# Reordering the first transfers of a fused convolution and MLP kernel: softmax weights first on their own queue, x split on ScalarE's queue, the band read in 128 rows

## The chip, the cores and the metric

The kernel runs on one core of a Trainium2 chip. The metric is device time in microseconds: 745.34 us before, the median of three runs (745.31 to 746.46). A profiled execution of the same kernel took 745.89 us; its span from the first to the last instruction is 743.8 us, so 2.09 us lie around the span. TensorE's mean granted clock in it was 0.989. All times within the span below come from that execution.

## What is computed

A lightweight causal convolution along the sequence, whose seven taps per head are a softmax of a small weight table, followed by a two-layer MLP with an ELU between:

```python
# x: (8, 4096, 192) f32; weight: (8 heads, 7)
w = softmax(weight, axis=-1)
x_pad = concat([zeros(B, 6, D), x], axis=1)
attn[b, s, h, :] = sum_k w[h, k] * x_pad[b, s + k, h, :]      # 24 channels per head
h = attn.reshape(32768, 192) @ w_in                            # w_in (192, 2048)
g = where(h > 0, h, exp(min(h, 0)) - 1)
out = g @ w_out                                                # w_out (2048, 192), out f32
```

## The kernel before

The 32,768 tokens are cut into 32 super-tiles of 1,024 tokens, each of two groups of 512. A super-tile's d_ff is cut into 16 blocks q of 128; n counts blocks over all super-tiles, and each block has a unit for each group (r = 0, 1). For a unit, TensorE makes h in three matmuls of 64 rows (line 755), ACT takes the exponential (582), GpSimd clamps it (541), DVE combines it with h into gT (650), and TensorE multiplies by w_out (778) into an accumulator that ACT evacuates (586).

From super-tile 1 on, the convolution is a matmul of windows of x (xg, 118 rows for 112 outputs: 112 plus six of padding) with a banded matrix Tm (line 728). Its results csb are transposed by a DMA of SP into att. Tm is made once: the zeros zw go to a DRAM tensor `band` of 128 rows x 8 heads x 134 columns (line 812), the seven taps are written along its diagonals (822), and it is read back at an offset of six columns (827). The order on SP's queue is written out: zeros, diagonal, then the copy of w_in's second part from the upper 64 partitions to the lower 64 (825), then Tm. Waits stand between them: zeros after all of x for the first super-tile (`s_xs`), diagonal after the zeros and after DVE's wprb, copy after w_in's second part (`s_w[1]`), Tm after the diagonal.

Super-tile 0 is started differently, so as not to wait for Tm. Its x is loaded in float32 as windows of 112 rows (xs) by three DMAs in `first_window`: group 0's first window of 106 rows (the six of padding are zeroed by DVE) and its other four on SP, and group 1's five on ACT. ACT casts xs to xb in three steps (line 562); TensorE transposes xb (691), DVE and ACT evacuate to xT, and TensorE multiplies xT by seven diagonal matrices, taps (706), which DVE makes from the softmax (619). DVE and ACT evacuate to att.

The softmax weights wq arrive by three small DMAs on SP, behind its two loads of x: twice 64 rows by channel (lines 798), once a broadcast to all rows (806). DVE subtracts the maximum (596, 598), ACT takes the exponential wex (558), DVE normalises (605 to 609) and makes taps. On ACT, wex stands ahead of the casts xb. GpSimd issues all other loads: w_in's first part in six DMAs, its second part in three, w_out's first half, xg of super-tile 1, w_out's second half and xg of super-tile 2.

A planner in Python gives TensorE's order: each item has a planned time, from a clock per group that is held to at least 1,160 ns per block at the start (`PACE0`), and the items are sorted by it. `WARM = (15, 2)` are fillers, matmuls of 128 x 512 zeros without use: 15 stand before the transposes, and before each of n = 1, 2 and 3 stand two. Their count does not enter the planned times. The first convolution stands at n = 5 (`EARLY_CONV`), the first multiplication by w_out at n = 4 (`EARLY_O`). The second unit of a block from n = 4 on waits for the copy of w_in (`s_wd`).

Of the kernel before, what the change touches and what calls it, by code (L numbers as in the profile page):

```python
# [15 lines left out]
D = 192  # L16
# [3 lines left out]
CW = 112  # L20
GS = 512
SUP = 2 * GS
PAD = KSIZE - 1
KW = CW + PAD
TW = P + PAD
NWIN = 5
# [8 lines left out]
O_AT = (12, 16)  # L35
CONV_AT = (14, 18, 23, 25)
QB = 2
WARM = (15, 2)
WCOLS = ((0, 4 * FC), (4 * FC, 16 * FC))
XP = 128  # L40
MM_H, MM_O, MM_C = 216.0, 82.5, 102.5
# [12 lines left out]
def bass_lightweight_conv__then__act_elu_kernel(  # L54
# [80 lines left out]
    def emit(lists):  # L135
        at = [0, 0]
        while True:
            ready = [
                rt
                for rt in range(2)  # L140
                if at[rt] < len(lists[rt])
                and (lists[rt][at[rt]][2] is None or lists[rt][at[rt]][2]())
            ]
            if not ready:
                assert all(at[rt] == len(lists[rt]) for rt in range(2))
                return
            rt = min(ready, key=lambda rt: (clock[rt], 1 - rt))
            took, issue, _ = lists[rt][at[rt]]
            at[rt] += 1
            issue()  # L150
            clock[rt] += took
            if len(ready) == 1 and at[1 - rt] < len(lists[1 - rt]):
                clock[1 - rt] = max(clock)

    def warm(count):
        what = ("w", len(plan) + 1)
        take_bank(what)
        freed[bank_of[what]] = max(clock)
        plan.append((max(clock) - AHEAD, what + (count,)))
        clock[:] = [max(clock)] * 2  # L160
# [37 lines left out]
    for n in range(NP):  # L198
        if 0 < n < EARLY_O[0]:
            warm(WARM[1])  # L200
        if n < UNTIL:
# [32 lines left out]
    emit(tail)  # L234
    pe_order += [("w", 0, WARM[0])] + start_up
    pe_order += [item for _, item in sorted(plan, key=lambda p: p[0])]
# [38 lines left out]
    band = nc.dram_tensor("conv_band", (P, HEADS, TW), BF16).ap()  # L275

    with ExitStack() as stack:
        def sbuf(name, shape, dt):
            return stack.enter_context(nc.sbuf_tensor(name, shape, dt))
# [4 lines left out]
        def sema(name):  # L284
            return stack.enter_context(nc.semaphore(name))

        xg = sbuf("xg", [P, NXB, 2 * NWIN, D], BF16)
        Tm = sbuf("Tm", [P, HEADS, CW], BF16)
# [4 lines left out]
        xs = sbuf("xs", [P, 2 * NWIN, D], FP32)  # L293
# [28 lines left out]
        s_xs = sema("s_xs")  # L322
# [65 lines left out]
            W(s_fa, a)  # L388
            W(s_fd, d)

        def first_window(eng, gr, w0, w1):
            skip = PAD if gr + w0 == 0 else 0
            eng.dma_start(
                xs[skip:CW, 2 * w0 + gr : 2 * w1 : 2, :],
                bass.AP(
                    tensor=x_flat.tensor,
                    offset=(gr * GS + w0 * CW - PAD + skip) * D,
                    ap=[[D, CW - skip], [CW * D, w1 - w0], [1, D]],
                ),
            ).then_inc(s_xs, 16)  # L400

# [5 lines left out]
        def transposed(j):  # L407
            return xT[:, j, :].rearrange("p (w c) -> p w c", c=CW), windows_of(j)

        def first_att(j, c0, c1):  # L410
            b = bank_of["d", j] + (j == 2 and c0 > 0)
            return att[:, 0, j, c0:c1], H[:, b, c0:c1]
# [9 lines left out]
        def conv_evac(W, m):  # L422

            s, u = divmod(m, CU)
            if s > 2:
                W(s_att[s % 2], att_need(s - 2))
            return (
                csb[0:CW, s % 2, :].rearrange("p (r h i) -> p h r i", h=HEADS, i=8)[
                    :, HU * u : HU * (u + 1), :, :
                ],  # L430
                H[0:CW, bank_of["c", m], :]
                .rearrange("p (h c) -> p h c", h=HU)[:, :, 0:UC]
                .rearrange("p h (r i) -> p h r i", i=8),
            )
# [11 lines left out]
        def out_evac(W, k, g):  # L446
            W(s_out[k % 2], 32 * (k // 2))
            W(s_fin[g], k + 1)
            return (
                osb[:, k % 2, g, :, :].rearrange("p k d -> p (k d)"),  # L450
                acc_of(k, g)[:, 0 : 2 * D],
            )
# [97 lines left out]
        @block.scalar  # L550
        def _scalar(a):
            W = Waits(a)
            first_window(a, 1, 0, NWIN)
            a.memzero(scr[:, 0:1]).then_inc(s_scr)
            W(s_scr, 1)
            a.activation(scr[:, 1:2], scr[:, 0:1], ACT.Exp)
            W(s_set, 2)
            a.activation(wex[:], wq2[:], ACT.Exp).then_inc(s_wex)  # L558
            W(s_xz, 1)
            W(s_xs, 48)  # L560
            for j in range(3):
                a.activation(  # L562
                    xb[0:CW, j, :, :].rearrange("p w (h i) -> p w h i", i=8),
                    xs[0:CW, :, :].rearrange("p w (h j i) -> p j w h i", j=3, i=8)[:, j, :, :, :],
                    ACT.Copy,
                ).then_inc(s_cast)
            for sem, count, ins in (
                (s_xt, 3, transposed(2)),
                (s_first, 1, first_att(0, 0, GS)),
                (s_first, 3, first_att(2, 0, GS // 2)),  # L570
            ):
                W(sem, count)
                a.activation(*ins, ACT.Copy).then_inc(s_fa)  # L573
            for item in act_order:
                if item[0] == "c":
                    m = item[1]
                    W(s_cv, m + 1 - CU)
                    a.activation(*conv_evac(W, m), ACT.Copy).then_inc(s_ce)  # L578
                elif item[0] == "h":
                    i = unit_at[item[1:]]  # L580
                    W(s_h, i + 1)
                    a.activation(  # L582
                        E[:, i % NE, :], H[:, bank_of[item], :], ACT.Exp
                    ).then_inc(s_exp)
                else:
                    a.activation(*out_evac(W, *item[1:]), ACT.Copy).then_inc(s_oev[item[2]])  # L586
            evacuated_by(W, NK - 1, 1)
            out_group(a, NK - 1, 1)
# [203 lines left out]
        @block.sync  # L792
        def _sync(sy):
            W = Waits(sy)
            first_window(sy, 0, 0, 1)
            first_window(sy, 0, 1, NWIN)
            for g in range(2):
                sy.dma_start(  # L798
                    wq[HP * g : HP * (g + 1), HEADS, :],
                    bass.AP(  # L800
                        tensor=weight.tensor,
                        offset=0,
                        ap=[[KSIZE, HEADS], [0, HP // HEADS], [1, KSIZE]],
                    ),
                ).then_inc(s_wq, 16)
            sy.dma_start(
                wq[:, 0:HEADS, :].rearrange("p h k -> p (h k)"),
                bass.AP(tensor=weight.tensor, offset=0, ap=[[0, P], [1, HEADS * KSIZE]]),
            ).then_inc(s_wq, 16)
            W(s_zw, 1)  # L810
            W(s_xs, 48)
            sy.dma_start(
                band[:, :, :].rearrange("p h t -> p (h t)"), zw[:, :]
            ).then_inc(s_band, 16)
            W(s_band, 16)
            W(s_set, 6)
            diagonal = bass.AP(
                tensor=band.tensor,
                offset=0,
                ap=[[HEADS * TW + 1, P], [TW, HEADS], [1, KSIZE]],  # L820
            )
            sy.dma_start(diagonal, wprb[:, :, :]).then_inc(s_band, 16)
            W(s_w[1], 48)
            c0, c1 = WCOLS[1]
            sy.dma_start(w_in[HP:P, :, c0:c1], w_in[0:HP, :, c0:c1]).then_inc(s_wd, 16)
            W(s_band, 32)
            sy.dma_start(
                Tm[0:KW, :, :], band[0:KW, :, PAD : PAD + CW]
            ).then_inc(s_band, 16)

            sync_work = []
            for m in range(2 * CU - 1, CU * NS, CU):
                sync_work.append((unit_at_conv[m], ("c", m)))
            sync_work += [(at, item) for at, item in evacs]
            for _, item in sorted(sync_work):
                if item[0] == "c":
                    transpose(sy, W, item[1] // CU)
                elif item[1:] != (NK - 1, 1):
                    evacuated_by(W, *item[1:])
                    out_group(sy, *item[1:])  # L840
            for b in range(2):
                sy.wait_ge(s_out[b], 32 * NS)
# [28 lines left out]
```

## Time and profile before

| | us |
|---|---|
| Median of three runs | 745.34 |
| Profiled execution | 745.89 |
| Its span | 743.8 |
| TensorE's matmuls busy | 722.5 (97%) |
| ACT busy | 676.6 (91%) |
| GpSimd busy | 668.4 (90%) |
| DVE busy | 639.5 (86%) |
| First h product starts | 23.60 |
| First convolution starts | 36.94 |

Each busy time is that of one engine over the span; the engines work beside each other, so that the times are not to be added. The page also cuts the span into 40 slices of 18.6 us, and the digit is the busy share in tenths. The first two slices are where TensorE is not full:

```profile
PE   4599999999999999999999999999999999999998
PEclk7889999999999999999999999999999999999999
DMA  9616534445653644553354655344456435544212
```

The issues of the start, in time order, as the timeline has them (start, length of the issue on its engine): x on SP 0.80 (two, 0.78 together) and on ACT 0.80 (0.40), wq 1.62 (two, 1.43 together) and 3.08 (0.46), zeros 7.92, diagonal 18.16, copy of w_in 19.01, Tm 25.06. GpSimd issues its loads without a pause from 1.45 to 11.9.

### The profile page before, as it was taken

How to read it: one execution, taken by the hardware profiler on the slowest of the kernel's cores; microseconds unless marked ns; L12 is line 12 of the kernel's file. 1: busy time of each engine (PE TensorE's matmuls, PEld its weight loads, DVE VectorE, ACT ScalarE, POOL GpSimd, SP SyncE). 2: the span in 40 equal slices, each digit the busy share in tenths (PEclk: the TensorE clock that was granted, in tenths of full speed). 3: DMA queues.
4: the chain of work that ended last, by engine and by line, in shares of the span. 5: the costliest groups of instructions: out<-in, count | busy, mean ns of one | idle time of the engine just before them, and what ended most of it. 6: DMA issues, size and time to landing. Idle time of an engine off the chain costs nothing.

```text
span 743.8 us, 27548 instructions
## 1 busy us (share of the span) xinstructions
PE 722.5 (97%) x11823; PEld 681.0 (92%) x11824; DVE 639.5 (86%) x1044; ACT 676.6 (91%) x1285; POOL 668.4 (90%) x1111
## 2 busy tenths in 40 slices
PE   4599999999999999999999999999999999999998
PEld 1268999999999999999999999999999999999997
DVE  2479889899988989898998998898999889898993
ACT  2389999999999999999999999999999999999993
POOL 5379999999999999999999999999999999999893
PEclk7889999999999999999999999999999999999999
DMA  9616534445653644553354655344456435544212
GB/s 164 92 25 84 89 53 84 82 83 83 94 68 65 93 73 92 84 94 60 70 95 71 94 84 91 54 82 83 82 84 94 68 64 93 75 91 82 69 33 65
DMA packets 135800, 59.23 MB, mean 80 GB/s; under 512 B 100900, under 2 KB 135166, under 8 KB 135678
## 3 DMA queue, kind: packets, MB, share of 16 engines
q1 hardware_dynamic: 90814, 39.86, 23.5%
q0 software_dynamic: 44016, 16.99, 22.3%
q8 instruction: 92, 1.51, 0.8%
q10 hardware_dynamic: 848, 0.63, 0.3%
q14 instruction: 30, 0.25, 0.1%
HBM read 35.07 MB, written 25.45 MB: 81 GB/s over the span
## 4 chain that ended last, share of the span: by engine, by line
PE 91%; DMA 4%; POOL 2%; ACT 1%; DVE 1%; SPq 0%; issue 0%; DVEq 0%
PE H L778 51%; PE H L755 36%; PE H L728 3%; DMA Tm<-conv_band 2%; DMA wq<-in_weight_dram 1%; POOL E L541 1%; DMA conv_band<-wprb 1%; ACT E L582 1%; DVE gT L650 1%; POOL xg L481 0%; ACT csb L578 0%; SPq L798 0%; DVE xT L628 0%; DVE taps L619 0%; ACT osb L586 0%
## 5 line engine op out<-in xcount | busy, mean ns | idle before, releaser
L650 DVE SCALAR_TENSOR_TENSOR gT<-E,H 128x512 f16<-128x512 f32 x1024 | 633.4, 681 | 74.8 <-POOL E L541 73.1
L778 PE MATMUL H<-w_out,gT 64*128 64x192 f16 x8192 | 684.6, 243 | 0.1
L755 PE MATMUL H<-att,w_in 64*128 64x512 bf16 x3072 | 682.6, 377 | 0.4
L541 POOL TENSOR_SCALAR E<-E 128x512 f32<-128x512 f32 x1024 | 607.2, 612 | 62.1 <-ACT E L582 50.8
L778 PEld LDWEIGHTS H<-w_out,gT 64*128 64x128 f16 x8192 | 625.7, 94 | 22.3 <-PE H L778 2.2
L582 ACT ACTIVATE E<-H 128x512 f32<-128x512 f32 x1024 | 593.7, 601 | 37.3 <-PE H L755 11.5
L755 PEld LDWEIGHTS H<-att,w_in 64*128 64x128 bf16 x3072 | 275.8, 93 | 6.9 <-issue 1.5
L728 PE MATMUL H<-xg,Tm 64*112 64x240 bf16 x496 | 93.4, 268 | 8.0 <-DMA Tm<-conv_band 7.4
L578 ACT ACTIVATE csb<-H 112x480 bf16<-112x480 f32 x124 | 69.8, 563 | 0.0
L728 PEld LDWEIGHTS H<-xg,Tm 64*112 64x112 bf16 x496 | 58.5, 127 | 12.1 <-DMA Tm<-conv_band 7.7
L586 ACT ACTIVATE osb<-H 128x384 f32<-128x384 f32 x127 | 61.7, 486 | 7.5 <-PE H L778 7.4
L481 POOL DMA_DIRECT2D xg<-in_x_dram x63 | 56.1, 895 | 0.2 <-issue 0.2
L596 DVE TENSOR_REDUCE wmx<-wq 128x9 f32<-128x63 f32 x1 | 0.2, 220 | 12.2 <-DMA wq<-in_weight_dram 12.2
L558 ACT ACTIVATE wex<-wq 128x63 f32<-128x63 f32 x1 | 0.3, 256 | 11.4 <-DVE wq L598 11.4
L691 PE MATMUL H<-ident,xb 112*128 112x112 bf16 x15 | 1.8, 293 | 7.8 <-ACT xb L562 7.8
L685 PE MATMUL H<-zw 128*128 128x512 bf16 x20 | 7.6, 539 | 1.7 <-DVE zw L593 1.5
L691 PEld LDWEIGHTS H<-ident,xb 112*128 112x128 bf16 x15 | 1.2, 134 | 8.6 <-issue 8.3
L685 PEld LDWEIGHTS H<-zw 128*128 128x128 bf16 x21 | 2.4, 129 | 6.1 <-issue 4.6
L641 DVE COPY osb<-H 128x384 f32<-128x384 f32 x1 | 0.6, 559 | 8.5 <-PE H L778 8.5
L706 PE MATMUL H<-xT,taps 128*128 128x512 bf16 (+1 forms) x28 | 6.3, 393 | 0.2 <-DVE xT L628 0.2
L706 PEld LDWEIGHTS H<-xT,taps 128*128 128x128 bf16 x28 | 3.0, 111 | 3.4 <-issue 2.1
L573 ACT ACTIVATE att<-H 128x512 bf16<-128x512 f32 (+1 forms) x2 | 1.0, 490 | 5.2 <-PE H L706 5.2
(25 smaller groups left out, 19.8 us busy)
## 6 DMA issues: line engine op xcount, KB each, us to landing
out_dram<-osb SPq DMA_DIRECT2D x127, 192.0 KB, 3.3
xg<-in_x_dram POOLq DMA_DIRECT2D x61, 240.0 KB, 5.1
w_out<-in_moe_w_out_dram POOLq DMA_DIRECT2D x2, 384.0 KB, 16.7
w_in<-in_moe_w_in_dram POOLq DMA_DIRECT2D x3, 192.0 KB, 7.2
w_in<-w_in SPq DMA_DIRECT2D x1, 576.0 KB, 8.8
att<-csb SPq DMA_TRANSPOSE x31, 4.2
xs<-in_x_dram ACTq DMA_DIRECT2D x1, 420.0 KB
w_in<-in_moe_w_in_dram POOLq DMA_DIRECT2D x6, 64.0 KB, 5.5
```

What stands on the lines that cost most here:

```text
L481: g.dma_start(xg[0:rows, b, 2 * w0 + gr : 2 * w1 : 2, :], src).then_inc(s_x[b][gr], 16)
L541: g.tensor_scalar(out=E[:, i % NE, :], in0=E[:, i % NE, :], scalar1=1.0, scalar2=0.0, op0=ALU.min, op1=ALU.max,).then_inc(s_clp)
L578: a.activation(*conv_evac(W, m), ACT.Copy).then_inc(s_ce)
L582: a.activation(E[:, i % NE, :], H[:, bank_of[item], :], ACT.Exp).then_inc(s_exp)
L586: a.activation(*out_evac(W, *item[1:]), ACT.Copy).then_inc(s_oev[item[2]])
L650: v.scalar_tensor_tensor(out=gT[:, s % NG3, q, u, :], in0=E[:, i % NE, :], scalar=1.0, in1=H[:, bank_of[item], :], op0=ALU.subtract, op1=A ...
L685: pe.matmul(H[:, bank, :], zw[:, 0:P], zw[:, 0:GS], start=True, stop=True)
L691: ins = pe.matmul(windows_of(j)[:, w, :], xb[0:CW, j, 2 * w : 2 * w + 2, :].rearrange("p g c -> p (g c)"), ident[0:CW, 0:CW], start=w in ( ...
L706: ins = pe.matmul(H[:, bank_of[item] + part, c0:c1], taps[:, tap, :], xT[:, j, tap + c0 : tap + c1], start=(tap == 0), stop=(tap == KSIZE ...
L728: ins = pe.matmul(H[0:CW, bank_of["c", m], 256 * q : 256 * q + UC], Tm[rows, h, :], xg[rows, s % NXB, :, CPH * h : CPH * (h + 1)].rearrang ...
L755: ins = pe.matmul(H[:, bank_of[item[:3]], :], w_in[HP * r : HP * (r + 1), j, FC * q : FC * (q + 1)], att[HP * r : HP * (r + 1), s % 2, j, ...
L778: ins = pe.matmul(acc_of(k, g)[:, D * kb : D * (kb + 1)], gT[HP * rt : HP * (rt + 1), t % NG3, q, g, t0 : t0 + P], w_out[HP * rt : HP * (r ...
```

## The change

The transfers of x all go to ACT's queue, in four DMAs instead of three: group 0's first window is split into 96 rows and 10 rows, the other four windows and group 1's five stay whole. The three loads of the weights thereby are the first on SP's queue. The two waits for x count four DMAs instead of three. Tm is read in all its 128 rows instead of 118; the matmuls still use 118. The fillers before n = 1, 2 and 3 are one each instead of two.

```diff
-WARM = (15, 2)
+WARM = (15, 1)
...
-        def first_window(eng, gr, w0, w1):
-            skip = PAD if gr + w0 == 0 else 0
+        def first_window(eng, gr, w0, w1, r0, r1):
             eng.dma_start(
-                xs[skip:CW, 2 * w0 + gr : 2 * w1 : 2, :],
+                xs[r0:r1, 2 * w0 + gr : 2 * w1 : 2, :],
                 bass.AP(
                     tensor=x_flat.tensor,
-                    offset=(gr * GS + w0 * CW - PAD + skip) * D,
-                    ap=[[D, CW - skip], [CW * D, w1 - w0], [1, D]],
+                    offset=(gr * GS + w0 * CW - PAD + r0) * D,
+                    ap=[[D, r1 - r0], [CW * D, w1 - w0], [1, D]],
                 ),
             ).then_inc(s_xs, 16)
...
         def _scalar(a):
             W = Waits(a)
-            first_window(a, 1, 0, NWIN)
+            first_window(a, 0, 0, 1, PAD, PAD + 96)
+            first_window(a, 0, 0, 1, PAD + 96, CW)
+            first_window(a, 0, 1, NWIN, 0, CW)
+            first_window(a, 1, 0, NWIN, 0, CW)
...
-            W(s_xs, 48)
+            W(s_xs, 64)
             for j in range(3):
...
         def _sync(sy):
             W = Waits(sy)
-            first_window(sy, 0, 0, 1)
-            first_window(sy, 0, 1, NWIN)
             for g in range(2):
...
             W(s_zw, 1)
-            W(s_xs, 48)
+            W(s_xs, 64)
             sy.dma_start(
                 band[:, :, :].rearrange("p h t -> p (h t)"), zw[:, :]
             ).then_inc(s_band, 16)
...
             sy.dma_start(
-                Tm[0:KW, :, :], band[0:KW, :, PAD : PAD + CW]
+                Tm[:, :, :], band[:, :, PAD : PAD + CW]
             ).then_inc(s_band, 16)
```

## The prediction, made before the changed kernel was run

> **What bounds the kernel now.** I read the page first (engine shares and slices), then the chain that ended last in order of time, then the waits of the first 60 us, the busy time in stretches, and last the packets of each DMA queue in stretches of a microsecond. Bulk first: the row of busy time from 100 to 700 us (columns: length, busy time and instruction count of PE, PEld, DVE, ACT, POOL, then PEclk, DMA share, GB/s):
>
> ```profile
> 100.00:700.00 600.00, 599.91 (x10095) 581.42 (x10092) 541.92 (x879) 577.11 (x1099) 566.81 (x939) 1.00 0.48 80
> ```
>
> TensorE is busy for 599.91 of 600 us at full clock. The change edits nothing there, so what it is worth is by how much it moves the point at which this stretch begins. The chain shows what that point waits for (start, length):
>
> ```profile
> 3.08 10.75 DMA wq<-in_weight_dram
> 15.43 1.23 DVE taps L619 x7
> 16.66 1.29 DVE xT L628 x2
> 18.16 6.89 DMA conv_band<-wprb
> 25.06 11.84 DMA Tm<-conv_band
> 36.94 0.44 PE H L728
> ```
>
> Thirty of the first 37 us are three transfers: the softmax weights until 13.83, the taps written into the band in HBM, and the band read back as Tm. The waits say the same from the engines' side (total, times, longest):
>
> ```profile
> DVE wmx L596 <- DMA wq<-in_weight_dram: 12.2, 1, 12.2
> ACT wex L558 <- DVE wq L598: 11.4, 1, 11.4
> PE H L691 <- ACT xb L562: 7.8, 1, 7.8
> PE H L728 <- DMA Tm<-conv_band: 7.4, 1, 7.4
> SPq L358 <- DMA xs<-in_x_dram: 4.3, 1, 4.3
> SPq L358 <- DVE wprb L629: 9.8, 1, 9.8
> ```
>
> x has landed at 7.92 (SP goes on then, with the band's zeros), yet ACT starts its casts xb only at 14.53: they stand behind wex in its queue, and wex waits for the weights. TensorE loses 7.8 us there and 7.4 us before its first convolution. Why do 32 KB of weights take 10.75 us? The packets of SP's hardware queue in 8:9, 9:10 and 10:11 us, and then in 30:37 us, when Tm is read (packets, MB, share of 16 engines):
>
> ```profile
> q1 hardware_dynamic: 24, 0.00, 1.7%
> q1 hardware_dynamic: 7, 0.00, 0.4%
> q1 hardware_dynamic: 5, 0.00, 0.4%
> ...
> q1 hardware_dynamic: 929, 0.21, 13.5%
> ```
>
> A share of 13.5% of 16 engines is 2.2 engines: Tm's 118 rows x 8 heads = 944 pieces of 224 B run on two engines, 472 each, 25 ns apiece. And from 8 to 11 us only 36 small packets crawl, while the software queue holds the engines (92 to 108% in the same answers).
>
> [...]
>
> **The change part by part.**
>
> *Weights ahead.* SP loses two x issues (0.37 + 0.35) and starts wq at 0.80: issues of 0.79, 0.60 and 0.46 end near 2.7. x issued at 0.80 had its first packets just before 2.0, so the last wq transfer starts near 3.8 [...]. GpSimd's data begins between 4 and 5 (19 packets in that microsecond). I take 4.8; bounds 4.3 and 7. Then wmx and wq2 (0.25 each), wex (0.29), wsum, wrs, wch (0.77) end at 6.4, taps (1.23) at 7.6. Before, taps ended at 16.66.
>
> *x on ACT.* Four issues of 0.40 plus gaps run from 0.80 to 2.5; they delay the table load (1.28) and two tiny steps to 4.2, hidden as wex can't start before 5.3. The transfers are 96 + 10 + 448 + 560 = 1,114 pieces on one queue. ACT's queue moved 380 pieces in 3:4 us before, so 2.9 us from 2.0: read at 4.9, landed at 6.0 (bounds 5.3, and 9 if it meets the weights). The wait for 64 instead of 48 only counts the fourth transfer. Behind it on ACT are xb, xT and the first att; on SP the zeros, the diagonal, the w_in copy and Tm.
>
> *The start that follows.* xb runs 6.0 to 8.0 (1.97 before). TensorE's 15 fillers end at 7.6 as before, so the transposes run 7.6 to 8.5, xT on DVE and ACT to 9.4, the 21 full-size tap products from 8.7. Before they took 6.31 us, half of it at clock 0.50 after idling; now the fillers have just ended, so 21 x 0.216 = 4.5 us, to 13.3 (at the old speed 15.0). First h product: 13.6, against 23.6. w_in's first part must be there; GpSimd issues its last DMA at 4.38 and the trace has 10.3 us to landing, 14.7[...]. So 13.6 to 14.7.
>
> *WARM 2 to 1.* Three 512-column fillers of 0.216 go. One n took 1.29 and ACT's two exponentials 1.08, so n = 1 to 3 gain up to 0.6 us. I count it as nothing, since a wait follows directly (below); if none did, 0.6. The planner ignores the count, so the order stays.
>
> *Band and Tm.* Zeros issued at 6.3 instead of 7.92; landed near 9.7. wprb follows xT on DVE: 9.7. Diagonal issued near 10.2; its 1,024 pieces of 14 B took 6.89; against the larger w_in packets I say landed at 17.7 (bounds 16 and 20). In SP's order the copy of w_in to the lower half stands between, waiting for w_in's second part: 19.0 in the trace. The first two of its three loads were counted at 11.6 and 12.65 (issued 4.92 and 5.45, 6.7 and 7.2 to landing); [...] I take 15 (bounds 13.5 and 19). The copy (0.71 to issue) moves behind the diagonal [...]: landed 21.5 (23.8 by its old 8.8). Tm is issued at 17.7 to 18.4: [...]. **Tm lands at 24.5**; bounds 21.2 (issue + 3.5, nothing in its way) and 27. [...]
>
> *The sum.* TensorE needs the copy for the second h of n = 4, the first half of w_out before it (21.1 before, less now), and xg of super-tile 1 (22.3 and 23.9 before) plus Tm at the first convolution. By pace it arrives there at 13.6 + 5 x 1.1 = 19 to 20; so DMA still decides, at 24.5 against 36.94: **12.4 us gained**. The clock is down after the wait as before, so no gain from it. 743.8 - 12.4 = 731.4 us of span; with the 2.09 outside it 733.5; the profiled 745.89 is 0.55 above the median, so 733.0 for the median.
>
> **The rivals.**
> 1. *Likeliest: the SP chain w_in, copy, Tm decides*, 21.5 to 27 around 24.5: 733.0, own range 730.5 to 735.5. Chance 0.57.
> 2. *No long wait remains.* Everything lands with the pace, conv from about 21 and with a clock kept up (about half of the 4.4 us at 0.50 from 36.94 saved): 15.9 to 18 gained, 727.5 to 729.5. [...] 0.13.
> 3. *The start doesn't move much, only Tm gets short.* w_in and w_out bound the start, because GpSimd's queue is full until 24 us [...]. Tm issued at 25.06 would land at 28.6, before TensorE asks at 29.6: the 7.4 us go and about 2.2 of cold clock: 735.7 to 738. 0.22.
> 4. *Tm is not spread after all*: 18 + 11.84 = 30 or a little more: gain 6.5, 738.8. 0.02.
> 5. *Slower: x caught on its single queue.* [...] xb then starts when x lands; each microsecond beyond 14.53 costs one, but the 7.4 us of Tm's wait are returned, so it decides from x at about 22 us, and at 26 would give 749. Against: 1,022 of the same 1,114 pieces had moved by 5 us. 0.04.
> 6. *Nothing measurable*, gains and delays even out at 745: 0.02.
>
> **How the numbers follow.** 0.2% is 1.5 us, about what a measurement tells from no change. Faster is 0.57 + 0.13 + 0.22 + 0.02 = 0.94, the same 0.02, slower 0.04. From 729.5 to 737.5 takes in the first case with both bounds and most of the third; outside lie most of case 2, a part of 3, and 4 to 6, about two tenths.
>
> **What would show it.** Right: DVE's wmx before 7 us, xb near 6, first h product near 14, TensorE's first convolution between 21 and 27 with Tm or the w_in copy as releaser, Tm landing within 8 us of issue, SP's queue near 16 engines while it moves, 100 to 700 us unchanged. Wrong: wmx still after 10 us; w_in's second part still at 19 [...]; a new wait at xs; a second wait after the first convolution that gives the gain back.

## The result, and the profile after

The changed kernel takes 737.45 us (median of four runs, 737.37 to 737.84) against 745.33 us for the kernel before beside it: a ratio of 0.9892, 95% interval 0.9875 to 0.9909, or 7.9 us. Its profiled execution took 737.50 us with a span of 735.4 us, 8.4 less than before. A second set of runs on another chip gave 737.08 us and 0.9885 (0.9870 to 0.9899), that is 8.5 us.

The slices of the page, now 18.4 us each, that answer to those shown of before:

```profile
PE   5899999999999999999999999999999999999998
PEclk8899999999999999999999999999999999999999
DMA  9725545345566435345436464534445634544212
```

In the rows of TensorE and its clock only the first two slices differ. The long stretch is what it was, in the row of 100 to 700 us of the changed kernel (columns as before):

```profile
100.00:700.00 600.00, 599.92 (x10095) 580.99 (x10090) 542.11 (x878) 577.01 (x1098) 566.00 (x938) 1.00 0.48 80
```

So the whole gain is a shift of the start. The first convolution begins at 28.91 in place of 36.94 us, 8.0 earlier, and the span is 8.4 shorter. How the start gets there is told by the chain that ended last in the changed kernel (its main pieces; start, length):

```profile
2.48 9.38 DMA xs<-in_x_dram
11.95 5.83 DMA conv_band<-zw
17.80 7.01 DMA conv_band<-wprb
24.82 4.04 DMA Tm<-conv_band
28.91 0.31 PE H L730
```

Read it beside the chain of before. There the weights ended first (13.83), then the diagonal went out at 18.16 and Tm at 25.06. Now x heads the chain, and the diagonal goes out at 17.80 and Tm at 24.82: these two have hardly moved. What has changed is Tm's own time, 4.04 in place of 11.84 us. Some of the waits of the changed kernel up to 60 us, first the engines', then those of SP's queue (total, times, longest):

```profile
DVE wmx L598 <- DMA wq<-in_weight_dram: 6.5, 1, 6.5
PE H L693 <- ACT xb L564: 6.1, 1, 6.1
ACT wex L560 <- DVE wq L600: 3.8, 1, 3.8
ACT xb L564 <- DMA xs<-in_x_dram: 3.0, 1, 3.0
PE H L757 <- DMA w_in<-w_in: 1.8, 1, 1.8
```

```profile
SPq L358 <- DMA xs<-in_x_dram: 9.1, 1, 9.1
SPq L358 <- DVE wprb L631: 2.7, 1, 2.7
SPq L822 <- DMA conv_band<-zw: 2.7, 1, 2.7
```

The weights are there at 8.19 (wmx starts then; 13.86 before), but the casts xb now wait for x itself, which lands at 11.95 and not at 7.92 as before. On SP, the wait for x grew from 4.3 to 9.1 us, and after wprb was ready the diagonal still waited 2.7 us for the zeros. Last, TensorE waits 1.8 us for the copy of w_in at n = 4; Tm lands 1.3 us after that wait ends. In between TensorE has work, so that what it loses here it loses to the copy. In the profile of the second set, where the first convolution began at 27.84, the diagonal went out at 16.95, Tm at 23.72, and the chain itself goes through the copy instead of the diagonal and Tm:

```profile
17.39 9.29 DMA w_in<-w_in
```

Tm is indeed spread. The line below is SP's hardware queue in 26 to 28 us of the changed kernel (packets, MB, share of 16 engines); 0.26 MB in 981 packets means that nearly all of them are Tm's pieces of 224 B. The share of 69.8% is 11.2 of 16 engines; before, it was 13.5%, 2.2 engines, while Tm was read. How far the read in 128 rows would spread, no trace of before showed; it was the author's estimate, and the share is what was measured:

```profile
q1 hardware_dynamic: 981, 0.26, 69.8%
```

### The profile page after: what moved, and what is told of

Its sections match the earlier page's. It is cut to its first block, busy times and chain, and to the rows that moved or that the text cites. A ratio compares the mean times of both kernels' runs of the same rounds, so it can differ in the third digit from the quotient of the medians.

```text
span 735.4 us, 27543 instructions
## 1 busy us (share of the span) xinstructions
PE 721.5 (98%) x11820; PEld 680.7 (93%) x11821; DVE 640.4 (87%) x1044; ACT 676.9 (92%) x1285; POOL 668.3 (91%) x1111
## 3 DMA queue, kind: packets, MB, share of 16 engines
q10 hardware_dynamic: 1444, 1.05, 0.7%
## 4 chain that ended last, share of the span: by engine, by line
PE 92%; DMA 4%; POOL 2%; ACT 1%; DVE 1%; ACTq 0%; issue 0%; DVEq 0%; SPq 0%
PE H L780 52%; PE H L757 37%; PE H L730 4%; POOL E L540 1%; DMA xs<-in_x_dram 1%; DMA conv_band<-wprb 1%; ACT E L584 1%; DMA conv_band<-zw 1%; DMA Tm<-conv_band 1%; DVE gT L652 1%; POOL xg L480 0%; ACT csb L580 0%; ACTq L392 0%; ACT osb L588 0%; DVE osb L643 0%
## 5 line engine op out<-in xcount | busy, mean ns | idle before, releaser
L580 ACT ACTIVATE csb<-H 112x480 bf16<-112x480 f32 x124 | 69.8, 563 | 0.0
L687 PE MATMUL H<-zw 128*128 128x512 bf16 x17 | 6.0, 508 | 1.5 <-DVE zw L595 1.5
L498 POOL DMA_DIRECT2D w_in<-in_moe_w_in_dram x9 | 5.2, 652 | 0.1
```

The costliest lines, as they stand in the source:

```text
L498: g.dma_start(w_in[HP * half : HP * (half + 1), j, c0:c1], bass.AP(tensor=moe_w_in.tensor, offset=8 * j * FF + c0, ap=[[CPH * FF, HEADS], ...
L687: pe.matmul(H[:, bank, :], zw[:, 0:P], zw[:, 0:GS], start=True, stop=True)
```

## The experiments

Twelve runs in three sets of four; one of them is the changed kernel again. Each set ran on one chip, with the kernel before beside it: medians of 745.87, 746.35 and 745.61 us. Ratios are to that kernel.

### Each half alone

The kernel before, with one line changed:

```diff
-                Tm[0:KW, :, :], band[0:KW, :, PAD : PAD + CW]
+                Tm[:, :, :], band[:, :, PAD : PAD + CW]
```

> The kernel before, with Tm read in 128 rows as the only edit. Theory A (the short read of Tm is the whole gain, the reordering of the start nets nothing): Tm issued near 25.0, landed near 29, first convolution near 29.6, time 737.4 within 0.8 of the changed kernel. Theory B (the reordering gives a part of its own): 739 to 741, and the first convolution after 30.5.

Measured: 738.61 us, ratio 0.9903 (0.9886 to 0.9919).

The changed kernel with the same line put back:

> The changed kernel, with Tm read in 118 rows as before. Theory A: Tm issued near 24.8, some 11.8 us to landing, first convolution near 36.7, time 745 within 0.8 of the kernel before. Theory B: 742 to 744.

Measured: 742.24 us, 0.9950 (0.9936 to 0.9965), as theory B had it. The first of the two runs lies between the theories in time (738.61), and with B by its first convolution. The chain of the first of these two kernels:

```profile
18.13 7.08 DMA conv_band<-wprb
25.22 6.26 DMA Tm<-conv_band
31.52 0.31 PE H L728
```

and of the second:

```profile
17.16 6.60 DMA conv_band<-wprb
23.78 8.90 DMA Tm<-conv_band
32.73 0.45 PE H L730
```

The short read of Tm alone is worth 7.3 us, the reordering with its single filler alone 3.6, both together 7.9 to 8.5 (the two sets), not 10.9: the two shorten the same wait. With Tm short and the old order, Tm took 6.26 us from issue where the changed kernel has 4.04, and the copy of w_in ahead of it on SP landed at 28.4 (18.62 + 9.8).

That the reordering nets nothing is refuted for Tm in 118 rows (3.6 us). On top of the short Tm it is less sure: the first convolution comes 2.6 to 3.7 us earlier (31.52 against 28.91 and 27.84), but the time is only 1.2 to 1.5 us less, by comparing 738.61 with 737.45 and 737.08, and the intervals of the ratios overlap. The run with the short Tm alone has two fillers in each place, the changed kernel one; reordered with two (below) the medians are 736.81 and 736.34, 1.8 to 2.3 us less.

### Why x became late

Two suspects were tried: GpSimd's software queue, and the weights' small pieces ahead on SP. The first was taken away by holding GpSimd's loads until x is there:

```diff
+            W(s_xs, 64)
             load_w_in(0, 0)
```

> The changed kernel, with GpSimd's loads held until x has landed. If the software queue's early packets are what makes x land at 11.95 in place of 7.92, x lands by 7 us here; if it is the weights' tiny pieces in SP's queue, or the single queue, x still lands after 9.5. The whole time is not the point: all weights come later, 742 to 750.

Measured, in a single execution: 742.88 us; x landed at 8.63, the weights at 7.09. The second was taken away by the same wait at the head of SP's queue, so that the weights follow x:

```diff
             W = Waits(sy)
+            W(s_xs, 64)
             for g in range(2):
```

> The changed kernel, with SP's three loads of the softmax weights held until x has landed. If the weights' tiny pieces are what makes x late, x lands by 7.5 us here, and the weights 6 to 8 us later; if it is the software queue or the single queue, x still lands after 9.5. Time 736 to 742.

Measured, in a single execution: 741.27 us; x landed at 8.36, the weights at 17.06. The last issue of x and its landing (start, length) in the first and in the second of these runs:

```profile
2.48 6.15 DMA xs<-in_x_dram
2.24 6.12 DMA xs<-in_x_dram
```

Both landings fall between the two that were expected. With either suspect away, x lands 3.2 to 3.5 us earlier than with both (11.86 by the chain; the engines go on at 11.95). The same opening repeats only to about 1 us: in the changed kernel twice, with Tm put back and in the two runs with two fillers (below), the wait for x ended at 10.93 to 11.95. Against the earliest of these, some 2.2 us remain. No run takes both suspects away. A third suspect stays open, that all of x is on one queue now: on two queues, with the weights behind it, it was there at 7.92 and 8.57 in the kernel before and with the short Tm alone, and at 6.25 with the split (below).

The packets of 3:4 us show where x loses time; ACT's queue (q10) carries it. The kernel before, where it carried five windows:

```profile
q10 hardware_dynamic: 380, 0.28, 87.2%
```

The changed kernel:

```profile
q10 hardware_dynamic: 51, 0.04, 46.6%
q0 software_dynamic: 57, 0.06, 40.7%
q1 hardware_dynamic: 5, 0.00, 0.4%
```

Without the software queue:

```profile
q10 hardware_dynamic: 70, 0.05, 46.1%
q1 hardware_dynamic: 64, 0.00, 2.9%
```

Without the weights ahead:

```profile
q10 hardware_dynamic: 172, 0.13, 61.2%
q0 software_dynamic: 41, 0.01, 17.6%
```

The share divided by the packets is what one packet of x takes: 0.872 x 16 us / 380 = 37 ns before, 146 ns in the changed kernel, 105 without the software queue, 57 without the weights ahead. In the kernel before, x had 1,022 of its pieces through by 5 us, 553 on ACT's queue and 469 on SP's, and the software queue began only between 4 and 5; in the changed kernel it begins before 3 us (78 packets in 2:3), in the middle of x.

What runs beside x in the same microsecond is not the whole reason. In 4:5 us of the changed kernel a packet of x takes 229 ns, though hardly anything else moves:

```profile
q10 hardware_dynamic: 41, 0.03, 58.7%
q0 software_dynamic: 9, 0.00, 3.1%
q1 hardware_dynamic: 39, 0.00, 1.9%
```

And without the software queue the shares of 3:4 add up to 49%, so the engines were not full either. Why a packet of x takes longer then isn't settled by these runs.

The weights are slow in either company: 7.1 us from their last issue with x landed and the software queue busy, and 4.7 us (from 2.35) beside x with the software queue empty.

### The split of x

SP's queue in 2:3 us, with the first window at its head, had 33 packets and 8.8% of 16 engines (1.4 engines) in the kernel before, 29 and 7.4% with the short Tm alone, and 85 and 28.6% (4.6 engines) in the run that comes next. Each of the two expectations below gives two sets of figures: first for the case that the 106 rows in one DMA hold back the weights and w_in, then for the case that they don't.

The kernel before with the short Tm and the split, but the old queues and the weights behind x (the new form of `first_window` and the waits for four loads, as in the change, are left out here):

```diff
-            first_window(sy, 0, 0, 1)
-            first_window(sy, 0, 1, NWIN)
+            first_window(sy, 0, 0, 1, PAD, PAD + 96)
+            first_window(sy, 0, 0, 1, PAD + 96, CW)
+            first_window(sy, 0, 1, NWIN, 0, CW)
```

> The kernel before with Tm in 128 rows and x's first window split into 96 and 10 rows, on the old queues: two loads of x ahead of the weights on SP, one on ACT. [...] the weights land by 11 us (13.8 before), w_in's second part by 17 (19.0), the first convolution comes by 28.5 and the time is 735 to 737.5. [...] weights and w_in as before and 738 to 739, as with the short Tm alone.

Measured: 738.77 us (737.23 to 740.14), 0.9897 (0.9878 to 0.9916). Two of the four executions took 737.2 and 737.6, two 739.9 and 740.1; the profile is of the longest. In it x was there at 6.25 (7.92 before), the weights at 12.87 (13.86) and w_in's second part, 11.9 us from its issue, by 17.96, when the copy went out (19.01). The first convolution came at 31.20, little before the 31.52 of the short Tm alone. The other way round, the changed kernel with the first window in one DMA of 106 rows (`first_window` and the waits for three loads as before the change):

```diff
-            first_window(a, 0, 0, 1, PAD, PAD + 96)
-            first_window(a, 0, 0, 1, PAD + 96, CW)
-            first_window(a, 0, 1, NWIN, 0, CW)
-            first_window(a, 1, 0, NWIN, 0, CW)
+            first_window(a, 0, 0, 1)
+            first_window(a, 0, 1, NWIN)
+            first_window(a, 1, 0, NWIN)
```

> The changed kernel with x's first window in 106 rows in one DMA, on ACT's queue, as the only thing undone. [...] w_in's second part back near 19, x later than 11.95, w_in copy and Tm 1 to 3 us later, time 738.5 to 741. If the split did nothing and the order of the queues does all: 737.5 within 0.6, w_in's second part near 16.

Measured: 739.67 us, 0.9911 (0.9897 to 0.9926). x landed at 9.95, 1.0 to 2.0 us earlier than in the two profiles with the split, the weights at 9.22, 1.0 to 1.6 later; Tm took 5.77 us from issue. By the ratios that is 1.4 to 1.9 us above the changed kernel, but the intervals overlap. So in the new order the split may help, and not by making x land sooner. In the old order its worth isn't measured: the medians differ by 0.2 us (738.77 and 738.61), the four executions by 2.9. In the old order's run the weights came 1.0 us and w_in's second part 1.05 us sooner than before, where nearly 3 and 2 were expected; so the 106 rows in one DMA account for about 1 us of their lateness.

### The zeros, the fillers and the late loads

The changed kernel without SP's wait for x ahead of the zeros:

```diff
             W(s_zw, 1)
-            W(s_xs, 64)
             sy.dma_start(
```

> The changed kernel without SP's wait for x ahead of the zeros, so that they go right after the weights. If the chain x, zeros, diagonal, Tm decides: the diagonal goes out when wprb is there (near 15 in place of 17.8), Tm lands 1.5 to 3 us earlier, first convolution 26.5 to 27.5, time 735 to 736.5. If the copy of w_in decides by itself: 737.5 within 0.5. If the zeros in the way make x later by 1 us or more, that comes back: 737 to 739.

Measured: 735.85 us, 0.9861 (0.9847 to 0.9876). Its chain:

```profile
14.80 7.04 DMA conv_band<-wprb
21.86 5.89 DMA Tm<-conv_band
27.79 0.31 PE H L730
```

The diagonal goes out 3.0 us earlier than in the changed kernel's first profile, as soon as wprb is there; x landed at 11.65, so the zeros did not delay it. Tm follows 3.0 us earlier, but stands behind the copy of w_in and takes 1.85 us longer, so that the first convolution comes at 27.79, against 28.91 and 27.84 in the two profiles of the changed kernel. The time is 1.2 to 1.6 us less, with intervals of the ratios that just overlap; part of it can be the clock, which stayed at full here (below). SP's longest wait of the start is now the one for wprb, 11.5 us. In the kernel's order DVE makes wprb after xT, hence after x, though wprb needs the softmax alone. Moving it ahead was not tried.

The fillers back to two in the changed kernel, on two chips; the second run beside the changed kernel itself:

> The changed kernel with two fillers again before n = 1, 2 and 3. If the wait for the copy of w_in takes in what the fillers cost: 737.5 within 0.4. If not: 0.6 us slower, 738.1. If the fillers keep the clock up over the wait: 736 to 737.

> The changed kernel once more, on the same chip as the next three, to set them against: 8 to 9 us below the kernel before. Theory A (the one filler lets the clock fall during the wait for the copy of w_in): clock 0.50 for about 4 us after the first convolution in the trace, mean clock 0.991 to 0.993.

> The changed kernel with two fillers before n = 1, 2 and 3, against it on one chip. Theory A: full clock after the first convolution, 0.8 to 1.6 us faster than the changed kernel. Theory B (the fillers have nothing to do with it, the copy of w_in lands at chance times): within 0.4 us of it.

Measured: 736.81 us, 0.9875 (0.9859 to 0.9892); then the changed kernel 737.08 (736.88 to 737.99), and with two fillers 736.34 (735.65 to 736.95), 0.9875 (0.9858 to 0.9892). The stretches of 28 to 30 and 30 to 32 us (PEclk is the third number from the end), first of the changed kernel's second profile, then with two fillers:

```profile
28.00:30.00 2.00, 2.00 (x16) 1.66 (x14) 1.02 (x2) 1.56 (x4) 1.33 (x3) 0.50 0.03 8
30.00:32.00 2.00, 1.91 (x16) 1.27 (x16) 1.50 (x3) 1.55 (x4) 1.23 (x3) 0.65 0.00 0
```

```profile
28.00:30.00 2.00, 1.75 (x23) 1.17 (x20) 1.16 (x2) 2.00 (x5) 1.77 (x3) 1.00 0.03 8
30.00:32.00 2.00, 1.91 (x25) 1.20 (x21) 1.96 (x4) 2.00 (x6) 1.56 (x3) 1.00 0.00 0
```

Both kernels waited for the copy (2.1 and 2.3 us) and began their first convolution at 27.84 and 27.64. In the first the clock then fell to half, 16 matmuls in the two microseconds in which the second did 23, and SP's next transpose went out at 36.76 against 35.51. That is 1.25 us, 0.2 of it from the earlier start. The medians differ by 0.74 us on one chip, with intervals of the ratios that overlap.

The number of fillers does not decide alone. With early zeros and one filler, after a wait of 1.5 us for Tm, the clock stayed up; with the split on the old queues and two fillers, after a wait of 2.6 us, it fell (in this order):

```profile
28.00:30.00 2.00, 1.76 (x23) 1.17 (x22) 1.49 (x4) 1.37 (x3) 1.16 (x2) 1.00 0.03 8
```

```profile
32.00:34.00 2.00, 2.00 (x17) 1.48 (x14) 0.61 (x1) 1.55 (x3) 0.93 (x2) 0.50 0.00 0
```

Still, the mean clock of each execution speaks for the fillers. All eight of the changed kernel have 0.991 to 0.993, six of the eight with two fillers 0.995 to 0.997. So with two fillers the clock stayed up in more of these executions; what that is worth in time stays near the scatter.

Then early zeros and two fillers together, and the same with w_out's second half and xg of super-tile 2 loaded from within GpSimd's first units:

```diff
-            load_w_out(1)
-            for gr in range(2):
-                load_x(2, gr)
             for i, (n, u) in enumerate(units):
...
+                if i == 4:
+                    load_w_out(1)
+                if i in (8, 10):
+                    load_x(2, i // 2 - 4)
                 W(s_exp, i + 1)
```

> The changed kernel with the zeros sent without waiting for x and two fillers. The chain gives 1.3 to 2 us for the zeros; of the fillers nothing more if the wait is short enough for the clock to stay up: 735 to 736, 1.5 to 2.5 below the changed kernel.

> As the run with early zeros and two fillers, and with w_out's second half and xg of super-tile 2 loaded only after GpSimd's first units. If the full software queue is what makes the diagonal, the copy and Tm slow: diagonal down to 5 us to landing, Tm landed by 25, no wait of TensorE over 1 us before the first convolution, 733.5 to 735. If these three are slow by themselves: 735 to 736 as without. If the late loads collide with the first units: slower than that run by up to 2 us.

Measured: 735.63 us (735.25 to 736.89), 0.9866 (0.9849 to 0.9882), the lowest median of its set, 1.45 us below the changed kernel, though the intervals still overlap. With the late loads 736.50, 0.9873 (0.9857 to 0.9889). There Tm was issued at 20.32 in place of 21.61, the copy took 7.5 us in place of 8.5 and Tm 3.3 in place of 6.1, so with the emptier software queue SP's transfers were faster in this profile. But the first convolution came only 0.7 us earlier and waited for something else, in the waits of that kernel:

```profile
PE H L731 <- DVE gT L653: 2.0, 3, 1.3
```

GpSimd's issues stand before its clamps, DVE waits for those and TensorE for DVE; they are on that kernel's chain, among them:

```profile
24.09 0.89 POOL w_out L509
27.35 0.85 POOL xg L480
```

What DMA gave back, GpSimd took.

## Why the prediction was right in time and wrong in its likeliest way

The change made the kernel faster, and the time fell into the range, but that it did is luck: 737.45 is 0.05 us inside the end at 737.5, and of the four executions one lies at that end and one beyond it. It was not the case that was called likeliest. The figure is that of the third rival, "The start doesn't move much, only Tm gets short" (735.7 to 738), but not for that rival's reason: w_in's second part came 3 us sooner than before (15.98 in place of 19.0). What happened is the chain of the first rival, in which copy and Tm decide, 4.4 us late because x was late. A late x was the fifth rival, with a chance of 0.04; x lost time already from 3 to 5 us. Against that rival the prediction set the 1,022 pieces moved by 5 us; 469 of them had been on SP's queue. Of its own signs, Tm's landing within 8 us (4.04), the many engines (69.8% of 16) and the unchanged stretch came; wmx, xb, the first h product and the first convolution were all late, and the new wait at xs, a sign of being wrong, was there.

1. *Weights ahead: 4.8, bounds 4.3 to 7.* They landed at 8.19. Their cost was the author's estimate, made as if nothing ran beside them. Held apart from the software queue they still needed until 7.09. The gain against before (5.7 us) was real but smaller than the 9.1 forecast.
2. *x on ACT: 6.0, bounds 5.3 to 9.* This is the step that failed. x landed at 11.95. The rate of 380 pieces in a microsecond was read from a stretch in which both hardware queues carried bulk rows of x and nothing else, and put on one queue beside the weights and the software queue. There x moved 51 and 41 pieces in the two microseconds from 3 to 5. Taking either away brings x at least 2.2 us sooner, but to 8.4 or 8.6, not to 6.0: the rest stays open. The bound of 9 "if it meets the weights" thought of company, but was too small.
3. *The start that follows: first h product 13.6 to 14.7.* It came at 21.30. The casts begin at 11.95, 5.95 later than predicted. The tap products then took 6.93 us, not 4.5: the fillers had not "just ended" but 6.1 us before the first transpose, and after that time without work the clock was at 0.50 from 14 to 18 us.
4. *Zeros at 6.3, diagonal at 10.2, w_in's second part at 15, Tm at 24.5.* The zeros hang on x, and went out at 11.95; the diagonal at 17.80. The second part of w_in landed at 15.98, close to what was said, but the copy could not use it: it stands behind the diagonal on SP, went out at 18.23 and landed at 27.43. Tm landed at 28.86. Tm's own time from issue, 6.1 to 6.8 in the prediction, was 4.04: the copy ahead of it had 2.6 us to go, and Tm landed 1.4 after it. The 24.5 was the author's estimate, and one size that it started from was misread. The 25 ns apiece for Tm's pieces are 11.84 us over 472, but Tm hardly moved before 30 us; the share of 13.5% over 30 to 37 us gives 7 x 16 x 0.135 / 929 = 16 ns.
5. *The 106 rows in one DMA.* That they hold back wq and w_in was the author's estimate; by the two runs on the split they are worth about 1 us and not the main cause.
6. *The fillers: counted as nothing, "a wait follows directly".* A wait did follow, but in both profiles of the changed kernel the clock fell to 0.50 after it; beside the run with two fillers the trace puts about 1 us on that. Here waits of 1.8, 2.1 and 2.6 us, with thin stretches around them, were followed by a clock of 0.50, and one of 2.3 us was not; at what idleness the clock falls isn't shown by these runs.
7. *The sum.* 12.4 us were forecast and 7.9 measured. Nearly all of the missing 4.5 us is the distance from 24.5 to 28.9. Along SP's chain it is made up of zeros issued 5.65 us late, because of x, and 1.95 us longer from there to the diagonal, less 0.5 for a shorter diagonal and 2.75 for a shorter Tm. Early zeros alone don't undo it, as wprb hangs on x too. The short Tm was the part that held, and its worth alone (7.3) is nearly the 7.4 us that the third rival gave it.

## What to carry to other kernels

A transfer's rate must be read from a stretch with the same company and the same queues: bulk rows that took 37 ns a piece beside each other on two queues took 146 ns on one, beside small pieces and a software queue. When one of two transfers is put ahead, ask which of them the other queues' work hangs on; here zeros, diagonal, copy and Tm all hung on x, which was the one that lost. And a DMA whose queue shows few engines while it moves is worth a look before any reordering: Tm's read had 13.5% of 16 engines in 118 rows and its queue 69.8% in 128, and the ten rows more gave 7.3 us alone, where the whole change gave 7.9 to 8.5.

## What the runs showed of the hardware that had not been expected

- The three loads of the weights, 32 KB in all in pieces of 28 and 224 B, took 4.7 us from their last issue with the software queue idle and 7.1 beside it. The 835 KB of x took 9.4 us from its last issue in the changed kernel, 6.1 with the weights behind it.
- The load of 10 rows took 0.85 us to issue on ACT while SP issued the weights, 0.61 while SP waited (the weights behind x). On SP, in the old order, no issue of x took over 0.41. So it isn't the ten rows alone.
- The zeros, 268 KB to DRAM, needed 5.83 us from issue in the changed kernel, and their first packets were seen only in 15:16 us, over 3 us after it.
- The same read of Tm in 118 rows (13.5% of 16 engines in 30 to 37 us of the kernel before) took 11.84 us from issue in one kernel and 8.90 in another, and in 128 rows 3.3 (with the late loads) to 11.0 (with GpSimd's loads behind x). In the longest it was issued 0.8 us after the copy of w_in, and TensorE's wait for that copy ended 8.9 us after the copy's issue.
